# Moving the next loads to GpSimd's queue and the casts into one block in a fused attention and mixer kernel

## The chip, the cores and the metric

The kernel runs on one core of a Trainium2 chip. The time is the device time of one execution in microseconds, the median of several runs. The engines are TensorE (PE: matmuls and transposes), VectorE (DVE), ScalarE (ACT), GpSimd (POOL) and SyncE (SP). In this kernel SP issues most of the transfers and GpSimd the rest. Each engine works through its own list of instructions in the order in which the program gives them, and waits on semaphores for the others.

## The reference

There are B = 8 batches, H = 8 heads, S = 576 positions of head width D = 64, so that the model width is 512. `global_idx` names 8 of the positions as global. Inputs and output are float32.

```python
scores = scale * np.matmul(q, k.transpose(0, 1, 3, 2))
mask = np.abs(pos[:, None] - pos[None, :]) <= window          # window = 32
mask = mask | is_global[:, None] | is_global[None, :]
scores = np.where(mask, scores, -1000000000.0)
attn = np.exp(scores - np.max(scores, axis=-1, keepdims=True))
attn = attn / (np.sum(attn, axis=-1, keepdims=True) + 1e-09)
x = np.matmul(attn, v)            # heads side by side: (B, S, 512)
# mixer: token MLP across positions (576 -> 256 -> 576), channel MLP (512 -> 1536 -> 512)
h = np.maximum(xt @ w_tok1, 0.0) @ w_tok2                      # xt = x.transpose(0, 2, 1)
u = x + h.transpose(0, 2, 1)
h2 = np.maximum(u @ w_ch1, 0.0) @ w_ch2
return u + h2
```

So every position attends to a band of 65 neighbours and to the 8 global positions, and the global positions attend to everything. The result goes through the two MLPs.

## The kernel before, in words

All operands of matmuls are float16. The eight heads are taken as four pairs `p`, and the 576 positions as five tiles, the last of them with 64. The work is written out in *periods*: `period(b)` does the channel MLP of batch `b` and, between its pieces, the attention and the token MLP of batch `n = b + 1`. It also prepares batch `m = b + 2`.

- **Channel MLP.** The list `dense` holds units. `M4(b, j)` (12 of them) is four matmuls of 128x512 into a PSUM tile of the pool `psm`, which has two buffers, and a ReLU on ACT (L628). After an odd `b` three units `M4l` follow, which do the short last tiles of two batches. `M5(b, tau, part)` is six matmuls (L651). Part 1 ends in an add on DVE that makes `osb` (L655, L658 for the short tiles), and SP stores that. `d(k)` takes `k` units from the list. What a period leaves of the list is the `tail`, which the next period's `scores` take first.
- **Scores.** `scores(p)` has score matmuls (`S_`, L431) in the PSUM pool `pss` of three buffers, three exps on ACT (L444, L457, L462), and the mask products `SM` on DVE (L473 and L479). Between them stand units of `dense`. For the periods up to n = 2 `T` transposes the q and k of pair `p + 2` on PE into a `pss` buffer, and `TE` copies them to `qT` and `kT` (L414 to L420, all on DVE). From n = 3 on the transposes are DMAs (`turns`, on SP) and `order` copies their result to `kT` (L356) and `qT` (L362) on DVE.
- **Global positions.** `gather` and `gather_t` (L308 to L316) collect the global rows. `globals_` (L378) copies them into the first columns of each tile of `qT`. `GK` (L488) does the scores of the global positions for all pairs and `OG` their value products. `PV(n, tau)` are the value products of a tile.
- **Token MLP.** `M1`, `M2`, then `M3`, which transposes `u` into `uT` by DMAs on SP (for batch 0 by PE).
- **Loads and casts.** `load(i)` brings q and k of a batch as float32: `load_rest` into `lr`, `load_qk` into `lq` and `lk`, of which there is one buffer each. `casts` are nine float16 copies of these into `rn` and `qk` (L332, L335): `rn` first, then q and k of each pair. `load_v16` loads v on GpSimd with a cast in the transfer.

The order of the work is that of the program text on each engine. Within a period from n = 3 on it is: scores of pairs 0 to 2, `GK`, the `turns` of batch `m`, `load(m + 1)`, scores of pair 3, `OG`, the value products with `M1` and the `order` copies of batch `m`, `load_v16(m)`, `M2` and `M3`, the first three casts of batch `n + 2`, two units, and `globals_(m)`. The next six casts stand in the next period, three after `scores(0)` and three after `scores(1)`:

```python
        scores(0)
        cast(m, 3, 6)
        d(1 if tail > 5 else 0)
        scores(1)
        cast(m, 6, 9)
        d(max(tail - 4 - (tail > 5), 0))
        scores(2)
        GK(n)
```

Periods n = 1 and n = 2 differ: `load(2)` and `load(3)` stand at their heads, the casts of batch 2 are one block at the end of n = 1, those of batch 3 stand on GpSimd behind `GK(2)`, and `load(4)` follows the `turns` of batch 3.

Of the kernel before, what the change touches and what calls it, by code (L numbers as in the profile page):

```python
# [18 lines left out]
WIN = 32  # L19
# [7 lines left out]
def kernel(  # L27
# [12 lines left out]
    nc = tc.nc  # L40
    B, H, S, D = q.shape
# [7 lines left out]
    LAST = S - P * (NT - 1)  # L49
# [13 lines left out]
    def psm(shape, dtype=F32, name="m"):  # L63
        return psM.tile(shape, dtype, tag="m", name=name)
# [18 lines left out]
        r1 = P - WIN if c == NT - 1 else P  # L83
        return r0, r1, P * c - WIN + r0

    def load_qk(b, hs):
        for ten, dst in ((q, lq), (k, lk)):
            nc.sync.dma_start(
                out=dst[:, hs].rearrange("p h i d -> p h (i d)"),
                in_=ten[b, hs, 0 : S - LAST, :].rearrange("h (p i) d -> p h (i d)", i=4),  # L90
            )

    def load_rest(b):
        for t, ten in enumerate((q, k)):
            nc.sync.dma_start(
                out=lr[LAST * t : LAST * t + LAST], in_=ten[b, :, S - LAST : S, :].rearrange("h p d -> p h d")
            )

# [230 lines left out]
    def cast_qk(b, ti, p, eng):  # L329

        if p is None:
            eng(out=rn.rearrange("p n (r d) -> p (n r) d", r=2), in_=lr)  # L332
        else:
            hs = slice(2 * p, 2 * p + 2)
            eng(out=qk[:, ti, p].rearrange("q i (r d) -> q r i d", r=2), in_=(lq, lk)[ti][:, hs])  # L335

    def casts(b, eng):
        return [lambda: cast_qk(b, 0, None, eng)] + [
            lambda ti=ti, p=p: cast_qk(b, ti, p, eng) for p in range(NP) for ti in range(2)
        ]  # L340
# [36 lines left out]
    def globals_(b):  # L377
        nc.vector.tensor_copy(  # L378
            out=qTs[b % 2][:, :, :, 0:NG], in_=gT[:, b].unsqueeze(2).to_broadcast([P, NP, NT, NG])
        )  # L380
# [28 lines left out]
    def TE(b, p):  # L409
        pT = st[b]["pT", p]  # L410
        qT, kT = qTs[b % 2][:, p], kTs[b % 2][:, p]

        pm = pT[:, 0, 0:512].rearrange("p (i t x) -> p t x i", i=4, t=4)
        nc.vector.tensor_copy(out=qT[:, 0:4, GW:QS].rearrange("p t (x i) -> p t x i", i=4), in_=pm)  # L414
        nc.vector.tensor_copy(out=qT[:, 4, GW : GW + LAST], in_=pT[:, 1, 512 : 512 + LAST])
        nc.vector.tensor_copy(  # L416
            out=kT[:, WIN : WIN + 512].rearrange("p (x i) -> p x i", i=4),
            in_=pT[:, 1, 0:512].rearrange("p (i x) -> p x i", i=4),
        )
        nc.vector.tensor_copy(out=kT[:, WIN + 512 : WIN + S], in_=pT[:, 1, 512 + LAST : 640])  # L420

    def S_(b, p, part):
        qf = qTs[b % 2][:, p].rearrange("p t x -> p (t x)")
# [44 lines left out]
    def S_all(b, p):  # L468
        return S_(b, p, 0) + S_(b, p, 1)
# [74 lines left out]
    def M1(b, ch):  # L544
        s = st[b]
        if ch == 0 and b == 0:
            s["a1p"] = [psm([P, 512], name=f"a1p_{b}_{tt}") for tt in range(2)]
        elif ch == 0:
            ps = pss([P, 2, 512], name=f"a1p_{b}")
            s["a1p"], s["a1pp"] = [ps[:, 0], ps[:, 1]], ps  # L550
        ps = s["a1p"]
        for tt in range(2):
            w = w1[:, ch, P * tt : P * tt + P] if ch < NT - 1 else w1l[:, b % 2, P * tt : P * tt + P]
            nc.tensor.matmul(ps[tt], lhsT=w, rhs=x16s[b % 2][:, ch, :], start=(ch == 0), stop=(ch == NT - 1))  # L554
        if ch < NT - 1:
            return
        a1 = mb.tile([P, 2, DM], F16, tag="a1", bufs=1, name=f"a1_{b}")
        if b == 0:
            nc.scalar.activation(out=a1[:, 0], in_=ps[0], func=AF.Relu)
            nc.vector.tensor_scalar(out=a1[:, 1], in0=ps[1], scalar1=0.0, scalar2=None, op0=ALU.max)  # L560
        else:
            nc.scalar.activation(out=a1, in_=s["a1pp"], func=AF.Relu)
        s["a1"] = a1
        s["u16"] = mb.tile([P, 4, DM], F16, tag="u16", name=f"u16_{b}")
        if b % 2 == 0:
            s["ul"] = mb.tile([P, DM], F16, tag="ul", name=f"ul_{b}")
        else:
            s["ul"] = st[b - 1]["ul"]
# [20 lines left out]
    def M23_first(tau):  # L589
        s = st[0]  # L590
        if tau == 0:
            s["uT"] = mb.tile([P, 4, 512], F16, tag="uT", name="uT_0")
        ps = psm([P, 512], name=f"hp0_{tau}")
        for ch in range(2):
            nc.tensor.matmul(
                ps, lhsT=w2[:, ch, P * tau : P * tau + P], rhs=s["a1"][:, ch, :], start=(ch == 0), stop=(ch == 1)
            )
        nc.vector.tensor_add(out=s["u16"][:, tau], in0=x16s[0][:, tau], in1=ps)
# [8 lines left out]
    def M3(b, part):  # L607
        s = st[b]
        if part == 0:
            s["uT"] = mb.tile([P, 4, 512], F16, tag="uT", name=f"uT_{b}")  # L610
        if part < 2:
            for i in range(2):
                tau = 2 * part + i
                nc.sync.dma_start_transpose(out=s["uT"][:, :, P * tau : P * tau + P], in_=s["u16"][:, tau, :])
        else:
            s["uTl"] = mb.tile([P, 4, P], F16, tag="uTl", name=f"uTl_{b}")
            nc.sync.dma_start_transpose(out=s["uTl"], in_=s["ul"])
# [46 lines left out]
    def d(k):  # L664
        for _ in range(k):
            if dense:
                dense.pop(0)()

    def load(i):
        if i < B:  # L670
            load_rest(i)
            load_qk(i, slice(0, H))

    def turns(i):
        turn_rest(i)
        for p in range(NP):
            turn(i, p)

    def cast(i, lo, hi):
        if 3 < i < B:  # L680
            for c in casts(i, nc.scalar.copy)[lo:hi]:
                c()

    def period(b):
        n, m = b + 1, b + 2
        odd = b % 2
        dense.extend(lambda j=j: M4(b, j) for j in range(NJ))
        if odd:
            dense.extend(lambda j=j: M4l(b, j) for j in range(3))
        dense.extend(lambda t=t, i=i: M5(b, t, i) for t in range(4 + odd) for i in range(2))  # L690
        if n == B:
            d(len(dense))
            return
        tail = len(dense) - (23 if odd else 20) - 2 * odd
        regular = n > 2

        def scores(p):
            es = S_all(n, p)
            es[0]()
            es[1]()  # L700
            d(1)
            es[2]()
            if n < 3 and p < 2:
                T(n, p + 2)
            d(1)
            SM(n, p)
            if n < 3 and p < 2:
                TE(n, p + 2)
            elif n > 2 and p < 2:
                order(n, p + 2)  # L710

        if n == 1:
            load(2)
        elif n == 2:
            load(3)
        scores(0)
        cast(m, 3, 6)
        d(1 if tail > 5 else 0)
        scores(1)
        cast(m, 6, 9)  # L720
        d(max(tail - 4 - (tail > 5), 0))
        scores(2)
        GK(n)
        if regular and m < B:
            turns(m)
            load(m + 1)
        if n == 2:
            for c in casts(3, nc.gpsimd.tensor_copy):
                c()
            turns(3)  # L730
            load(4)
        d(1)
        scores(3)
        d(1)
        OG(n)
        d(1)
        if n == 3:
            gather_t(1)
        fill = [order_rest, lambda i: order_k(i, 0), lambda i: order_q(i, 0), lambda i: order_k(i, 1), lambda i: order_q(i, 1)]
        for tau in range(NT):  # L740
            PV(n, tau)
            if 0 < tau < 4:
                M1(n, tau - 1)
            if regular and m < B:
                fill[tau](m)
            if tau < 4:
                d(1)
        M1(n, 3)
        d(len(dense) - (8 + 2 * odd))
        M1(n, 4)  # L750
        d(1)
        if m < B:
            load_v16(m)
        M2(n, 0)
        M3(n, 0)
        M2(n, 1)
        M3(n, 1)
        M2(n, 2)
        if n % 2:
            M3(n, 2)  # L760
        if n == 1:
            for c in casts(2, nc.scalar.copy):
                c()
            d(2)
            T(2, 0)
            TE(2, 0)
            T(2, 1)
            TE(2, 1)
        else:
            cast(n + 2, 0, 3)  # L770
            d(1)
            if n == 2:
                order_rest(3)
                order(3, 0)
                order(3, 1)
            d(1)
        if m < B:
            globals_(m)

    def cast0(p):  # L780
        cast_qk(0, 0, p, nc.scalar.copy)
# [58 lines left out]
        M1(0, tau - 2)  # L840
    M1(0, NT - 2)
    M1(0, NT - 1)
    M23_first(0)
    M23_first(1)
    M3_first(0)
# [7 lines left out]
    T(1, 1)  # L853
    TE(1, 0)
    TE(1, 1)
    gather_t(0)
    globals_(1)
    qk_pads(1)
    pads(1)
    load_wc2(0)  # L860
# [36 lines left out]
```

## Time and profile before

| | |
|---|---|
| median of 3 runs | 349.94 us (348.34 to 350.1) |
| the profiled execution | 347.81 us |
| its span | 346.1 us |
| granted TensorE clock, mean | 0.982 |
| PE busy | 302.6 us (87%) |
| DVE busy | 200.6 us (58%) |
| ACT busy | 165.3 us (48%) |
| GpSimd busy | 72.3 us (21%) |

The span is what the trace covers; the execution's time includes what lies around it. In the trace's views a row of a timeline gives start, duration, engine, line and operation, then `out<-in`, the shapes, a count, and in brackets the idle time just before with what ended it. A row of the waits gives the waiting operation, what it waited for, and microseconds in all, times and the longest one. A row of the windows gives, for a stretch, its length, the busy time of PE, PE's weight loads, DVE, ACT and GpSimd with their counts, the granted clock, the DMA share and the rate in GB/s. Line numbers are those of the kernel before; the batch of a period is told from the time. S(n, p) stands for the score matmuls of batch n and pair p, e0(n, p) for their first exp, kT(n, p) and qT(n, p) for the copies, T(n, p) for the transposes on PE.

### The profile page before, as it was taken

The numbers are of one execution on the slowest core, as the hardware profiler recorded it, in microseconds if no ns is written. First come the engines' busy times: TensorE is split into PE (matmuls) and PEld (weight loads), VectorE is DVE, ScalarE is ACT, GpSimd is POOL, SyncE is SP. The second block draws the span as 40 slices with busy tenths as digits, with TensorE's granted clock in tenths as the row PEclk, the third lists the DMA queues.
The fourth block names the chain that finished last, engine by engine and source line by source line (L and its number), as shares of the span: only waits on it lengthen the run. The fifth ranks groups of instructions, "written<-read, shape, count | busy, mean of one in ns | idle before, by whom it ended". The sixth has DMA issues, their size and how long they took to land.

```text
span 346.1 us, 6451 instructions
## 1 busy us (share of the span) xinstructions
PE 302.6 (87%) x2541; PEld 157.8 (46%) x2541; DVE 200.6 (58%) x433; ACT 165.3 (48%) x292; POOL 72.3 (21%) x113
## 2 busy tenths in 40 slices
PE   1556859997989979999899999997899999998994
PEld 0334435553436634464346544643356445543641
DVE  5898767648396456675757456763763666351021
ACT  2438137605482346732973577335945247303600
POOL 8879535100069100040004000310000000000000
PEclk9999989999899989999999999999999999999998
DMA  5999999603889992599549964999350421033013
GB/s 156 255 294 155 225 247 196 39 32 91 239 186 127 228 229 76 108 127 296 150 112 134 290 128 102 112 226 238 93 93 17 110 77 30 0 76 123 0 63 91
DMA packets 114526, 48.18 MB, mean 139 GB/s; under 512 B 89408, under 2 KB 109760, under 8 KB 114496
## 3 DMA queue, kind: packets, MB, share of 16 engines
q1 hardware_dynamic: 77008, 39.60, 49.3%
q0 software_dynamic: 37200, 8.16, 29.1%
q8 instruction: 20, 0.33, 0.4%
q14 instruction: 10, 0.08, 0.1%
q10 hardware_dynamic: 288, 0.01, 0.0%
HBM read 36.12 MB, written 9.44 MB: 132 GB/s over the span
## 4 chain that ended last, share of the span: by engine, by line
PE 62%; DVE 16%; DMA 9%; ACT 7%; SPq 3%; issue 2%; ACTq 0%; DVEq 0%
PE op L651 21%; PE b1p L625 18%; DMA lk<-in_k_dram 8%; PE a1p L554 4%; PE s L431 3%; PE b1lp L638 3%; DVE e_all L479 3%; PE hp L578 3%; ACT e_all L444 3%; PE pv L531 2%; PE pv L522 2%; PE pv L527 2%; DVE kT L416 2%; ACT b L628 1%; ACT e_all L457 1%
## 5 line engine op out<-in xcount | busy, mean ns | idle before, releaser
L625 PE MATMUL b1p<-uT,wc 128*128 128x512 f16 x384 | 96.1, 383 | 5.4 <-DVE osb L655 4.3
L651 PE MATMUL op<-wc,b 128*128 128x512 f16 x384 | 90.8, 389 | 0.0
L628 ACT ACTIVATE b<-b1p 128x512 f16<-128x512 f32 x96 | 58.5, 609 | 64.9 <-PE b1p L625 64.6
L651 PEld LDWEIGHTS <-b 128*128 128x128 f16 x384 | 37.2, 99 | 45.8 <-issue 3.4
L625 PEld LDWEIGHTS <-wc 128*128 128x128 f16 x384 | 34.9, 98 | 48.5 <-issue 10.9
L655 DVE TENSOR_TENSOR osb<-u,op 128x512 f32<-128x512 f16 x32 | 21.9, 685 | 53.5 <-PE op L651 50.2
L324 POOL DMA_DIRECT2D vsh<-in_v_dram x35 | 29.9, 865 | 103.9 <-PE pv L531 101.1
L444 ACT ACTIVATE e_all<-s 128x832 f16<-128x832 f32 x32 | 27.8, 869 | 39.4 <-issue 20.6
L479 DVE TENSOR_TENSOR e_all<-e_all,bandm 128x1040 f16<-128x1040 f16 x64 | 43.7, 723 | 1.2
L584 DVE TENSOR_TENSOR u<-x,hp 128x512 f16<-128x512 f16 x28 | 17.4, 682 | 22.1 <-PE hp L578 22.1
L431 PE MATMUL s<-qT,kT 64*128 64x208 f16 (+1 forms) x320 | 20.9, 257 | 10.4 <-DVE qT L378 6.3
L539 DVE TENSOR_TENSOR x<-pv,rr 128x512 f16<-128x512 f32 (+1 forms) x40 | 27.6, 691 | 1.4
L522 PEld LDWEIGHTS <-e_all 128*128 128x128 f16 x320 | 22.1, 100 | 5.5 <-issue 0.5
L473 DVE TENSOR_TENSOR eg<-e_all,bandm 128x160 f16<-128x160 f16 x32 | 7.8, 245 | 28.8 <-ACT e_all L462 28.6
L522 PE MATMUL pv<-vsh,e_all 128*128 128x66 f16 x320 | 24.4, 197 | 0.0
L431 PEld LDWEIGHTS <-kT 64*128 64x128 f16 x320 | 12.5, 98 | 25.2 <-issue 16.1
L335 ACT CAST qk<-lq 128x512 f16<-128x512 f32 x28 | 17.8, 634 | 12.3 <-DMA lq<-in_q_dram 12.2
L457 ACT ACTIVATE e_all<-s 128x576 f16<-128x576 f32 x32 | 21.0, 657 | 3.2 <-PE s L431 3.2
L538 DVE RECIPROCAL rr<-pv 128x8 f32<-128x8 f32 (+1 forms) x40 | 8.3, 207 | 23.1 <-PE pv L531 22.9
L527 PE MATMUL pv<-vsh,e_all 128*128 128x66 f16 x256 | 21.1, 198 | 0.0
L335 ACT CAST qk<-lk 128x512 f16<-128x512 f32 x24 | 15.3, 638 | 11.6 <-DMA lk<-in_k_dram 11.6
L527 PEld LDWEIGHTS <-e_all 128*128 128x128 f16 x256 | 17.9, 101 | 3.5 <-issue 0.2
(154 smaller groups left out, 348.4 us busy)
## 6 DMA issues: line engine op xcount, KB each, us to landing
out_dram<-osb SPq DMA_DIRECT2D x32, 256.0 KB, 2.3
lq<-in_q_dram SPq DMA_DIRECT2D x7, 1024.0 KB, 7.4
lk<-in_k_dram SPq DMA_DIRECT2D x7, 1024.0 KB, 10.3
wc<-in_moe_w_ch_dram POOLq DMA_DIRECT2D x6, 512.0 KB, 12.9
vsh<-in_v_dram POOLq DMA_DIRECT2D x21, 128.0 KB, 5.8
vsh<-in_v_dram POOLq DMA_DIRECT2D x14, 96.0 KB, 6.2
lq<-in_q_dram SPq DMA_DIRECT2D x4, 256.0 KB, 5.3
lk<-in_k_dram SPq DMA_DIRECT2D x4, 256.0 KB, 5.7
```

Source lines behind the costliest of these rows:

```text
L324: nc.gpsimd.dma_start(out=vsh[b % 2][r0:r1, c, :, 0:D], in_=v[b, :, j0 : j0 + (r1 - r0), :].rearrange("h p d -> p h d"),)
L335: eng(out=qk[:, ti, p].rearrange("q i (r d) -> q r i d", r=2), in_=(lq, lk)[ti][:, hs])
L431: nc.tensor.matmul(ps[:, par, off : off + n], lhsT=kT[r, P * c : P * c + P], rhs=qf[r, lo : lo + n], start=True, stop=True,)
L444: nc.scalar.activation(out=e2[:, :, 1:3, 64:EW], in_=ps[:, :, 0 : 2 * W].rearrange("p h (c x) -> p h c x", c=2), func=AF.Exp, scale=scale,)
L457: nc.scalar.activation(out=o, in_=ps[:, :, 0 : 2 * QS].rearrange("p h (c x) -> p h c x", c=2), func=AF.Exp, scale=scale)
L479: nc.vector.tensor_mul(out=eh, in0=eh, in1=bandm)
L522: nc.tensor.matmul(o, lhsT=e_all[:, h, tau, EW - P - sh : EW - sh], rhs=vsh[b % 2][:, tau, h, :], start=hh == 0, stop=False,)
L527: nc.tensor.matmul(o, lhsT=e_all[:, h, tau + 1, 0:P], rhs=vsh[b % 2][:, tau + 1, h, :], start=False, stop=False)
L539: nc.vector.tensor_tensor(out=x16s[b % 2][r, tau, :].rearrange("p (f h x) -> p f h x", f=2, h=NP), in0=pq[r, :, :, 0:D], in1=rr[r].unsquee ...
L625: nc.tensor.matmul(ps, lhsT=wc1[:, cc, P * j : P * j + P], rhs=s["uT"][:, cc, :], start=(cc == 0), stop=(cc == 3))
L628: nc.scalar.activation(out=s["b1"][:, j, :], in_=ps, func=AF.Relu)
L651: nc.tensor.matmul(ps, lhsT=w, rhs=wc2[:, j, :], start=(j == 0), stop=(j == NJ - 1))
```

## The change

- Loads of q and k from batch 2 on are issued by GpSimd instead of SP. From n = 3 on `load(n + 2)` stands at the head of the period, ahead of the scores; before, it stood behind `GK` and the `turns`.
- The nine casts of batch `n + 2` stand in one block on ACT behind `M2` and `M3`. The casts of batch 2 (n = 1) stay where they were, those of batch 3 stay on GpSimd.
- `globals_(m)` moves from the end of the period to behind the value products, ahead of `M1(n, 3)`. `gather_t(0)` and `globals_(1)` move from behind the copies of batch 1's pairs 0 and 1 to ahead of `M23_first(0)`.
- The units of `dense` that stood behind `scores(0)` and `scores(1)` are taken inside `scores`, as `d(1 + k)` ahead of `SM` and of `TE` or `order`. The order on PE is the same; on DVE the `osb` add of such a unit comes ahead of the mask products and the copies.
- In `TE` the two `kT` copies of batches 1 and 2 are done by ACT instead of DVE.

```diff
--- before.py
+++ after.py
@@ -83,16 +83,16 @@
         r1 = P - WIN if c == NT - 1 else P
         return r0, r1, P * c - WIN + r0
 
-    def load_qk(b, hs):
+    def load_qk(b, hs, eng=None):
         for ten, dst in ((q, lq), (k, lk)):
-            nc.sync.dma_start(
+            (eng or nc.sync).dma_start(
                 out=dst[:, hs].rearrange("p h i d -> p h (i d)"),
                 in_=ten[b, hs, 0 : S - LAST, :].rearrange("h (p i) d -> p h (i d)", i=4),
             )
 
-    def load_rest(b):
+    def load_rest(b, eng=None):
         for t, ten in enumerate((q, k)):
-            nc.sync.dma_start(
+            (eng or nc.sync).dma_start(
                 out=lr[LAST * t : LAST * t + LAST], in_=ten[b, :, S - LAST : S, :].rearrange("h p d -> p h d")
             )
 
@@ -410,14 +410,15 @@
         pT = st[b]["pT", p]
         qT, kT = qTs[b % 2][:, p], kTs[b % 2][:, p]
 
+        copy_k = nc.vector.tensor_copy if b == 0 else nc.scalar.copy
         pm = pT[:, 0, 0:512].rearrange("p (i t x) -> p t x i", i=4, t=4)
         nc.vector.tensor_copy(out=qT[:, 0:4, GW:QS].rearrange("p t (x i) -> p t x i", i=4), in_=pm)
         nc.vector.tensor_copy(out=qT[:, 4, GW : GW + LAST], in_=pT[:, 1, 512 : 512 + LAST])
-        nc.vector.tensor_copy(
+        copy_k(
             out=kT[:, WIN : WIN + 512].rearrange("p (x i) -> p x i", i=4),
             in_=pT[:, 1, 0:512].rearrange("p (i x) -> p x i", i=4),
         )
-        nc.vector.tensor_copy(out=kT[:, WIN + 512 : WIN + S], in_=pT[:, 1, 512 + LAST : 640])
+        copy_k(out=kT[:, WIN + 512 : WIN + S], in_=pT[:, 1, 512 + LAST : 640])
 
     def S_(b, p, part):
         qf = qTs[b % 2][:, p].rearrange("p t x -> p (t x)")
@@ -668,18 +669,13 @@
 
     def load(i):
         if i < B:
-            load_rest(i)
-            load_qk(i, slice(0, H))
+            load_rest(i, nc.gpsimd)
+            load_qk(i, slice(0, H), nc.gpsimd)
 
     def turns(i):
         turn_rest(i)
         for p in range(NP):
             turn(i, p)
-
-    def cast(i, lo, hi):
-        if 3 < i < B:
-            for c in casts(i, nc.scalar.copy)[lo:hi]:
-                c()
 
     def period(b):
         n, m = b + 1, b + 2
@@ -694,7 +690,8 @@
         tail = len(dense) - (23 if odd else 20) - 2 * odd
         regular = n > 2
 
-        def scores(p):
+        def scores(p, k):
+
             es = S_all(n, p)
             es[0]()
             es[1]()
@@ -702,35 +699,27 @@
             es[2]()
             if n < 3 and p < 2:
                 T(n, p + 2)
-            d(1)
+            d(1 + k)
             SM(n, p)
             if n < 3 and p < 2:
                 TE(n, p + 2)
             elif n > 2 and p < 2:
                 order(n, p + 2)
 
-        if n == 1:
-            load(2)
-        elif n == 2:
-            load(3)
-        scores(0)
-        cast(m, 3, 6)
-        d(1 if tail > 5 else 0)
-        scores(1)
-        cast(m, 6, 9)
-        d(max(tail - 4 - (tail > 5), 0))
-        scores(2)
+        load(2 if n == 1 else 3 if n == 2 else n + 2)
+        scores(0, tail > 5)
+        scores(1, max(tail - 4 - (tail > 5), 0))
+        scores(2, 0)
         GK(n)
         if regular and m < B:
             turns(m)
-            load(m + 1)
         if n == 2:
             for c in casts(3, nc.gpsimd.tensor_copy):
                 c()
             turns(3)
             load(4)
         d(1)
-        scores(3)
+        scores(3, 0)
         d(1)
         OG(n)
         d(1)
@@ -745,6 +734,8 @@
                 fill[tau](m)
             if tau < 4:
                 d(1)
+        if m < B:
+            globals_(m)
         M1(n, 3)
         d(len(dense) - (8 + 2 * odd))
         M1(n, 4)
@@ -758,24 +749,23 @@
         M2(n, 2)
         if n % 2:
             M3(n, 2)
+        later = 2 if n == 1 else n + 2
+        if later < B:
+            for c in casts(later, nc.scalar.copy):
+                c()
         if n == 1:
-            for c in casts(2, nc.scalar.copy):
-                c()
             d(2)
             T(2, 0)
             TE(2, 0)
             T(2, 1)
             TE(2, 1)
         else:
-            cast(n + 2, 0, 3)
             d(1)
             if n == 2:
                 order_rest(3)
                 order(3, 0)
                 order(3, 1)
             d(1)
-        if m < B:
-            globals_(m)
 
     def cast0(p):
         cast_qk(0, 0, p, nc.scalar.copy)
@@ -840,6 +830,8 @@
         M1(0, tau - 2)
     M1(0, NT - 2)
     M1(0, NT - 1)
+    gather_t(0)
+    globals_(1)
     M23_first(0)
     M23_first(1)
     M3_first(0)
@@ -853,8 +845,6 @@
     T(1, 1)
     TE(1, 0)
     TE(1, 1)
-    gather_t(0)
-    globals_(1)
     qk_pads(1)
     pads(1)
     load_wc2(0)
```

## The prediction

> **What bounds the kernel now.** I read the page first: the busy shares, then the chain that ended last by engine.
>
> ```profile
> span 346.1 us, 6451 instructions
> PE 302.6 (87%) x2541; PEld 157.8 (46%) x2541; DVE 200.6 (58%) x433; ACT 165.3 (48%) x292; POOL 72.3 (21%) x113
> PE 62%; DVE 16%; DMA 9%; ACT 7%; SPq 3%; issue 2%; ACTq 0%; DVEq 0%
> ```
>
> TensorE (PE) is busy for 302.6 of 346.1 us, so the kernel is PE-bound with 43.5 us of gaps, and an edit is worth what it takes from or adds to those gaps, plus PE time at a low clock. The profiled execution took 347.81 us, 1.71 around its span; the median of the runs is 349.94, 2.13 above it. I sum against 347.81 and add 2.13 at the end. About 0.5% (1.75 us) is what a measurement here can tell from no change. Next I took the waits of PE, the windows by stage and the transfers in the chain:
>
> ```profile
> PE s L431 <- DVE qT L378: 6.3, 5, 2.7
> PE b1p L625 <- DVE osb L655: 4.3, 3, 1.6
> 200.00:228.00 28.00, 27.86 (x241) 14.02 (x240) 18.64 (x38) 17.07 (x33) 4.19 (x5) 1.00 0.81 118
> 154.21 10.12 DMA lk<-in_k_dram
> 226.70 11.18 DMA lk<-in_k_dram
> ```
>
> The first two rows (in all, times, longest) are waits that the diff touches: score matmuls waiting for the global columns (L378), and a channel-MLP unit waiting for a PSUM tile that a late `osb` add holds. The window row shows the other side: in the undisturbed period n=5 PE idles 0.14 of 28 us, so any new wait there is paid in full. The last two rows (issue, us to landing) say that the K load of periods 4 and 6 is itself in the chain.
>
> **Part 1: early loads and casts in one block (gain, n=4 and n=6).** ACT is in order. Before, the casts for the batch next but one stand there ahead of the exps of the period's first scores, and wait for a load issued late in the period before:
>
> ```profile
> 164.41 0.62 ACT L335 CAST qk<-lk 128x512 f16<-128x512 f32 x1 [2.79 <-DMA lk<-in_k_dram]
> 161.92 0.57 PE L431 MATMUL s<-qT,kT 64*128 64x208 f16 x10 [0.24 <-DVE qT L378]
> 165.84 0.39 PE L431 MATMUL s<-qT,kT 64*128 64x144 f16 x6 [0.36 <-ACT e_all L444]
> 173.26 1.02 PE L625 MATMUL b1p<-uT,wc 128*128 128x512 f16 x4 [1.57 <-DVE osb L655]
> 239.39 0.39 PE L431 MATMUL s<-qT,kT 64*128 64x144 f16 x6 [1.77 <-ACT e_all L444]
> 246.82 1.02 PE L625 MATMUL b1p<-uT,wc 128*128 128x512 f16 x4 [1.57 <-DVE osb L655]
> ```
>
> With the load issued at the head of period n, a whole period (about 35 us, from 161.92 to 234.07 are two) lies before its casts; the rows gave it 10 to 11. The casts then stand behind the token MLP, 9 x 0.52 (spacing of neighbouring casts) = 4.7 us, over before the next exps. The stalls on ACT go, and so does the 1.57, since the exps, the mask products and the `osb` adds are no longer late: n=4 gives 0.24 + 0.36 + 1.57 = 2.17, n=6 gives 0.24 + 1.77 + 1.57 = 3.58 (its 0.24 is the row below; it belongs to the moved global columns). Sum -5.75, between -3.3 (the two 1.57 and the 0.24s stay or turn into another wait) and -5.75. Nothing in n=5 and n=7, which have no such idles.
>
> **Part 2: global columns earlier (gain, n=2 and n=3).**
>
> ```profile
> 234.07 0.57 PE L431 MATMUL s<-qT,kT 64*128 64x208 f16 x10 [0.24 <-DVE qT L378]
> 123.22 0.57 DVE L356 COPY kT<-raw 128x512 f16<-128x512 f16 x1
> 124.22 0.19 DVE L378 COPY qT<-gT 128x160 f16<-128x160 f16 x1
> 124.45 0.57 PE L431 MATMUL s<-qT,kT 64*128 64x208 f16 x10 [2.26 <-DVE qT L378]
> 124.96 5.75 PE L651 MATMUL op<-wc,b 128*128 128x512 f16 x18
> 239.72 4.06 PE L651 MATMUL op<-wc,b 128*128 128x512 f16 x18
> ```
>
> At n=3 the first scores need pair 0 alone, whose copies end as pair 1's start (123.22, with some 0.1 of overlap); the columns at 124.22 stood behind both of pair 1's copies. Earlier columns let S(3,0) start about 1.15 sooner (124.45 - 123.30). The idle left is then 2.26 - 1.15 = 1.11, and the 18 matmuls behind it should run in 4.06 as at 239.72, not 5.75: another 1.69. Sum -2.84, between -1.15 and -2.84.
>
> A row and a rule on the clock: the idles of 2.26 (and 2.67, below) are followed by slow matmuls, the 1.77 at 239.39 is not, so the edge here lies between 1.77 and 2.26. The Trainium skill ("TensorE: Matmul & The Clock Gate", Part 1 and "HAM oscillation") has half clock only past about 3.4 us of idling, in a free-running window. By that rule the 1.69 would not be the idle's doing and would stay, -1.15 instead of -2.84; the rows differ from it, and I go by the rows.
>
> **Part 3: batches 1 and 2, K copies on ACT (loss).** In TE the K copies go from DVE to ACT, behind a wait for the DVE copies from the same PSUM tile; what queues behind them on ACT are the next exps and ReLUs, for which PE waits.
>
> ```profile
> 48.82 0.23 PE L309 MATMUL pg<-ident,g_q 128*128 128x128 f16 x1 [2.89 <-DVE g_q L308]
> 50.05 0.94 PE L431 MATMUL s<-qT,kT 64*128 64x208 f16 x10 [0.87 <-DVE qT L378]
> 45.17 0.68 DVE L587 TENSOR_TENSOR ul<-x,hp 64x512 f16<-64x512 f16 x1 [1.10 <-PE hp L578]
> 45.77 0.67 DVE L414 COPY qT<-pT 128x512 f16<-128x512 f16 x1
> 46.47 0.67 DVE L416 COPY kT<-pT 128x512 f16<-128x512 f16 x1
> 47.07 0.17 DVE L420 COPY kT<-pT 128x64 f16<-128x64 f16 x1
> 54.22 1.31 DVE L479 TENSOR_TENSOR e_all<-e_all,bandm 128x1040 f16<-128x1040 f16 x2
> 55.09 0.86 ACT L444 ACTIVATE e_all<-s 128x832 f16<-128x832 f32 x1
> 50.60:64.90 14.30, 14.02 (x110) 6.45 (x110) 8.56 (x20) 12.33 (x23) 7.23 (x8) 0.90 1.61 157
> ```
>
> Head of batch 1: the gather and the columns leave their place ahead of S(1,0) and go ahead of batch 0's `u`. That chain waits for PE here and there (1.10 before `ul`), so of the stretch that the gather takes now (48.82 to 50.05, 1.2) I let 0.8 through. Pair 0's Q copies then start at 45.77 + 0.8 and take 0.70 (to 46.47), its K copies on ACT 0.77 (46.47 to 47.24) and a hand-over of 0.1: S(1,0) at about 48.15 instead of 50.05, -1.9 (between 0 and the two idles' 3.76).
>
> Scores of batch 1: SM(1,0) ends on DVE at 54.22 + 1.31 = 55.5 and the Q copies 0.70 to 0.8 later, 56.3. Before, ACT went on with the next exp at 55.09; now it has kT(1,2) first and stands 1.2 longer, with the 0.7 of idle it had there 1.9. For kT(1,3) the same, 1.85. The two K pairs are about 0.8 each on ACT. That makes 1.9 + 1.85 + 1.6 = 5.3 us on an engine that in this window had 14.30 - 12.33 = 1.97 idle: +3.3, less the 1.9 head start. Net +1.4; up to +3.2 if the short PE idles that it brings (0.95 to 1.9) lower the clock. I take +2.1.
>
> ```profile
> 86.73 0.19 DVE L378 COPY qT<-gT 128x160 f16<-128x160 f16 x1
> 86.98 0.57 PE L431 MATMUL s<-qT,kT 64*128 64x208 f16 x10 [2.67 <-DVE qT L378]
> 87.48 2.63 PE L651 MATMUL op<-wc,b 128*128 128x512 f16 x6
> 90.87 1.55 PE L651 MATMUL op<-wc,b 128*128 128x512 f16 x6
> 92.45 0.69 DVE L655 TENSOR_TENSOR osb<-u,op 128x512 f32<-128x512 f16 x1 [5.53 <-PE op L651]
> 93.72 0.61 PE L405 MATMUL pT<-ident,qk 128*128 128x128 f16 x8
> ```
>
> Batch 2: S(2,0) no longer waits for the columns at 86.73 and the copies split on two engines: 85.45, -1.53; its following 6 matmuls in 1.55 rather than 2.63, -1.08. All later work of PE would come 2.6 earlier. But kT(2,2) on ACT now follows `osb` (92.45 - 2.6 = 89.9), SM (1.5), the Q copies (0.7) and is 0.8 itself: with the add's 0.6 it ends at 93.5, and the transposes T(2,3) need the PSUM buffer that it frees. PE reaches them at 93.72 - 2.6, some 91.2, and idles 2.3. The gain is spent there. Then kT(2,3) holds ACT in the same way behind SM(2,1), and the exps of pair 2 come some 1.8 late, part of it hidden. Net +1.0 by the value products, between -1.5 and +3.
>
> **Part 4: extra output units ahead of the mask products (loss, n=3 to 7).** `d(1 + k)` puts the tail's `osb` adds ahead of SM and `order` on DVE. The fourth pair of GK's matmuls waits for the second `order` copy.
>
> ```profile
> 206.85 0.69 DVE L655 TENSOR_TENSOR osb<-u,op 128x512 f32<-128x512 f16 x1 [1.98 <-PE op L651]
> 209.46 0.60 DVE L362 COPY qT<-raw 128x512 f16<-128x512 f16 x1
> 209.33 0.57 PE L431 MATMUL s<-qT,kT 64*128 64x208 f16 x10
> 211.66 0.36 PE L488 MATMUL gk<-qT,kgz 128*32 128x384 f16 x4
> ```
>
> From the start of an `osb` to the end of that copy: 209.46 + 0.60 - 206.85 = 3.21. Now this chain begins when the last output unit ends on PE (T0, here about 209.4) plus 0.2, and ends at T0 + 3.4; PE wants GK's fourth pair at T0 + 2.3 to 2.6 (211.66 is T0 + 2.3, three of its matmuls first). A stall of about 0.83 (0.83 to 1.1) in each of five periods, in which PE has no slack: +4.2 (4.2 to 5.5; 0 if DVE starts the add earlier than PE's modelled end). It's a wait that before is not there at all.
>
> **Part 5: the queue.** 24 load issues leave SP for Pool. Pool's v loads bound their price.
>
> ```profile
> L324 POOL DMA_DIRECT2D vsh<-in_v_dram x35 | 29.9, 865 | 103.9 <-PE pv L531 101.1
> ```
>
> Four issues of 0.87 are 3.5 us a period on an engine that waits 100 us; load(n+2) waits there for the casts of n+1, and only load_v16 queues behind it, not wanted for a period. So the issue costs nothing; without that cover it would be 3.5 a period. What changes is the company: the loads (10.12 and 11.18 to landing above) now run beside the `uT` transposes and the output stores at a period's start. I add +0.5 (0 to +4: `uT` is issued about 6 us or more ahead of its use).
>
> **Sum.** 347.81 - 5.75 - 2.84 + 2.1 + 1.0 + 4.2 + 0.5 = 347.0; on the median's level 349.1, -0.2%.
>
> **Rivals.**
> R1, faster: the new waits are covered. The `order` chain of part 4 needs to be only 0.8 us quicker, and DVE idles nearby (1.98 before the `osb`). Without part 4, 344.9; with batches 1 and 2 near their lower ends too, 343. Against: the chain is made of rows.
> R2, slower: the clock. Part 3 makes idles of 1.85 to 2.3 where the trace's edge is 1.77 to 2.26. If they count as long, each costs 1.69 as at 124.96: three of them +5.1, 354.2. It decides from about 2 us of idle. For: 2.3 is past 2.26. Against: the windows' clock already dips to 0.90 there with little idle.
> R3, slower: the loads on Pool land late or hold up `uT`. The new bound is then the end of +4: 352.6. For: 11.18 us for one transfer before. Against: a period to land. A page bears on this: the Trainium skill ("DMA: Bandwidth & Descriptors", "SWDGE vs HWDGE vs iDMA") says that GpSimd's descriptors are written to SBUF state from which VectorE's two-port modes lock it out, and that SP's are immune. By that rule the issues would stretch; the v rows' 0.87 beside a DVE busy 58% don't show it.
> R4, it doesn't do what it says: the DMA waits on ACT come back because a load waits for its buffer: part 1 is lost, 354.8.
>
> **How the numbers follow.** Forecast as summed 0.45, R1 0.22, R2 0.18, R3 0.10, R4 0.05. The forecast's own range, from the bounds of parts 1 to 4 taken half to each side, is 346.5 to 352. Of its 0.45, 0.13 lies under 348.2 (0.5% faster), 0.25 between, 0.07 above 351.7. Faster: 0.22 + 0.13 = 0.35. Same: 0.25 and 0.02 of R3 = 0.27. Slower: 0.07 + 0.18 + 0.08 + 0.05 = 0.38. The range of 8 in 10 runs from half of R1 to R2: 344.0 to 354.5.
>
> **What would show it.** In the changed profile: no cast on ACT waiting for a load in n=4 and n=6; no score matmul waiting for L378's global columns; 18 matmuls behind S(3,0) in about 4.06; a new wait of GK's matmuls for the `order_q` copy, 0.8 a period; ACT's K copies waiting for DVE in batches 1 and 2 and PE transposes waiting for them. Wrong would be: no wait at GK (then R1), PE clock under 0.9 between 85 and 117 us (R2), matmuls of `uT` waiting for a transfer (R3), casts still waiting (R4).

## The result and the profile after

The changed kernel takes 362.39 us (median of 4 runs, 361.49 to 362.76) against 350.02 for the kernel before (4 runs, 348.34 to 351.37). The ratio is 1.0352 with a 95% interval of 1.0303 to 1.0401: slower by 3.5%, outside the range of the forecast. The profiled execution took 361.49, its span is 359.8, 13.7 more than before. The page of the changed kernel, its busy shares and the chain that ended last:

```profile
span 359.8 us, 6482 instructions
PE 307.7 (86%) x2541; PEld 158.9 (44%) x2541; DVE 194.4 (54%) x417; ACT 171.7 (48%) x308; POOL 92.5 (26%) x137
PE 63%; DVE 17%; DMA 8%; ACT 5%; issue 4%; SPq 2%; DVEq 0%; ACTq 0%
```

PE has 52.1 us of gaps instead of 43.5, and 5 us more of busy time for the same 2541 matmuls, which is a lower clock (granted 0.962 in the mean, 0.982 before). Its waits say where (what waits, for what; us in all, times, longest):

```profile
PE b1p L626 <- issue: 4.9, 1, 4.9
PE b1p L626 <- DVE osb L656: 4.3, 3, 2.4
PE b1p L626 <- DMA uT<-u: 3.3, 1, 3.3
PE b1p L626 <- ACT b L629: 2.7, 2, 1.3
PE gk L489 <- ACT kT L421: 1.9, 2, 1.1
PE gk L489 <- DVE qT L362: 1.7, 3, 0.6
PE s L432 <- DVE qT L362: 1.2, 1, 1.2
```

No row has L378, the global columns, any more, and no cast ahead of the scores' exps holds PE up. In their place the first channel-MLP matmuls (L626) wait. The third row names the transposed `u`. The first says "issue", but the view of the line that issues those transposes (L615) puts the same wait on the weight load ahead of that matmul, and gives the landing times:

```profile
  PEld L626: 5.1, 1
  PE b1p L626: 3.3, 1
DMA to landing us min/median/max: 2.4/2.6/10.6
```

So PE waits twice for `uT`, in periods 2 and 4. Two long transfers stand in the chain of the changed kernel (start, us):

```profile
169.23 10.61 DMA uT<-u
214.11 8.46 DMA out_dram<-osb
```

The timeline of its PE shows what ended behind them, with the idle time in brackets:

```profile
97.85 1.86 PE L626 MATMUL b1p<-uT,wc 128*128 128x512 f16 x4 [4.88 <-issue]
179.97 1.87 PE L626 MATMUL b1p<-uT,wc 128*128 128x512 f16 x4 [3.33 <-DMA uT<-u]
223.41 3.56 PE L626 MATMUL b1p<-uT,wc 128*128 128x512 f16 x8 [2.40 <-DVE osb L656]
```

Its timelines of SP and GpSimd at the first of these places:

```profile
83.43 5.93 SPq L615 DMA_TRANSPOSE uT<-u  x4
86.03 0.90 POOL L88 DMA_DIRECT2D lq<-in_q_dram  x1 [2.24 <-ACT qk L335]
86.91 0.89 POOL L88 DMA_DIRECT2D lk<-in_k_dram  x1
```

And its timeline of DVE at the third:

```profile
222.67 0.69 DVE L656 TENSOR_TENSOR osb<-u,op 128x512 f32<-128x512 f16 x1 [4.70 <-DMA out_dram<-osb]
```

GpSimd comes to a load at the moment when ACT's cast block has freed the buffers, and that block stands next to `M3`, so the load starts while the `uT` transposes are under way (83.43 on SP, 86.03 on GpSimd). The last transpose of period 2 is issued at 87.44 and takes 10.3 to land; PE wants it at 92.97 (97.85 - 4.88). Late landings as such are not new. In the kernel before, the view of the same line (L614) has

```profile
DMA to landing us min/median/max: 2.4/3.4/8.4
```

but there no matmul waits for them. In period 5 the last `uT` lands as late (issued at 211.87, 10.0), but what ends PE's wait is an `osb` add held up by an output store that takes 8.46: the three `osb` buffers are full, DVE waits 4.70 for one, and PE waits for the PSUM tile that DVE would free. Behind each of these three idles of 2.4 to 4.9 the matmuls are slow: 1.86 or 1.87 for 4 and 3.56 for 8, where 1.02 and 1.90 are usual.

### The profile page after: what moved, and what is told of

Same layout as the page of the kernel before. It is cut to its first block, busy times and chain, and to the rows that moved or that the text cites. A ratio compares the mean times of both kernels' runs of the same rounds, so it can differ in the third digit from the quotient of the medians.

```text
span 359.8 us, 6482 instructions
## 1 busy us (share of the span) xinstructions
PE 307.7 (86%) x2541; PEld 158.9 (44%) x2541; DVE 194.4 (54%) x417; ACT 171.7 (48%) x308; POOL 92.5 (26%) x137
## 3 DMA queue, kind: packets, MB, share of 16 engines
q0 software_dynamic: 41040, 22.32, 38.9%
## 4 chain that ended last, share of the span: by engine, by line
PE 63%; DVE 17%; DMA 8%; ACT 5%; issue 4%; SPq 2%; DVEq 0%; ACTq 0%
PE b1p L626 20%; PE op L652 19%; PE a1p L555 4%; PE hp L579 4%; DVE e_all L480 4%; DMA out_dram<-osb 4%; PE b1lp L639 3%; DMA uT<-u 3%; PE pv L523 3%; PE s L432 3%; PE pv L532 3%; PE pv L528 2%; ACT e_all L445 2%; DVE osb L656 2%; DMA lk<-in_k_dram 2%
## 5 line engine op out<-in xcount | busy, mean ns | idle before, releaser
L626 PE MATMUL b1p<-uT,wc 128*128 128x512 f16 x384 | 102.6, 404 | 15.9 <-issue 4.9
L652 PE MATMUL op<-wc,b 128*128 128x512 f16 x384 | 87.9, 379 | 0.0
L626 PEld LDWEIGHTS <-wc 128*128 128x128 f16 x384 | 36.7, 102 | 62.9 <-issue 28.4
L480 DVE TENSOR_TENSOR e_all<-e_all,bandm 128x1040 f16<-128x1040 f16 x64 | 42.6, 707 | 1.2
L95 POOL DMA_DIRECT2D lr<-in_q_dram x6 | 4.3, 713 | 95.3 <-ACT rn L332 95.3
L555 PE MATMUL a1p<-x,w 128*128 128x512 f16 x64 | 18.9, 379 | 0.0
```

Of the source, the lines that this page charges most:

```text
L480: nc.vector.tensor_mul(out=eh, in0=eh, in1=bandm)
L626: nc.tensor.matmul(ps, lhsT=wc1[:, cc, P * j : P * j + P], rhs=s["uT"][:, cc, :], start=(cc == 0), stop=(cc == 3))
L652: nc.tensor.matmul(ps, lhsT=w, rhs=wc2[:, j, :], start=(j == 0), stop=(j == NJ - 1))
```

## The experiments

The twelve runs start from the changed kernel (`a_`, `d_`) or from the kernel before (`b_`). Ratios are to the kernel before, run on the same chip; spans, waits and landings are those of one profiled execution of each kernel. What the table shows is worked out from the starts of S(n,0) in the timeline of PE: the length of each period, with what the prediction's steps make of it if part 5 (the +0.5) is left out.

| us | before | forecast without part 5 | changed | a_noload | a_dvek_noload |
|---|---|---|---|---|---|
| head, to S(1,0) | 50.05 | 48.15 | 48.72 | 48.65 | 49.17 |
| n=1 | 36.93 | 39.4 | 39.99 | 38.86 | 33.72 |
| n=2 | 37.47 | 38.9 | 43.21 | 39.67 | 34.60 |
| n=3 | 37.47 | 36.4 | 36.47 | 36.47 | 36.47 |
| n=4 | 37.14 | 36.0 | 41.78 | 35.80 | 35.81 |
| n=5 | 35.01 | 35.6 | 38.83 | 35.71 | 35.70 |
| n=6 | 38.54 | 36.0 | 35.81 | 35.80 | 35.80 |
| from S(7,0) | 73.49 | 74.3 | 74.99 | 74.34 | 74.13 |
| span | 346.1 | 344.8 | 359.8 | 345.3 | 335.4 |

**a_noload: what do the loads cost?**

```diff
-        if i < B:
+        if i < 3:
             load_rest(i, nc.gpsimd)
```

> The changed kernel without the loads of q and k of batches 3 to 7 (what was loaded last is cast again; that part of the data is left out). It prices everything that these loads cost beside other transfers. Theory 1: 12 to 16 us faster than the changed kernel, 346 to 350: no wait of PE for uT in periods 2 and 4, none for an osb add in 5. Theory 3 (the K copies on ACT and the order of DVE): at most 4 us faster, over 358.

347.88 us, ratio 0.9963 (0.9937 to 0.9989); span 345.3, 14.5 less than the changed kernel. The waits of its PE have no row for `uT`, and an `osb` add holds PE 1.0 us in all:

```profile
PE b1p L626 <- ACT b L629: 3.5, 4, 1.3
PE gk L489 <- DVE qT L362: 2.9, 5, 0.6
PE b1p L626 <- DVE osb L656: 1.0, 1, 1.0
```

Theory 1 holds: at their new place the loads cost 14.5 us, most of it in periods 1, 2, 4 and 5 of the table (1.1, 3.5, 6.0 and 3.1). PE is busy 302.9 us here, so 4.8 of the 14.5 are slower matmuls and 9.7 are gaps. The run leaves the loads out altogether; it prices the loads at this place and on this queue, and doesn't tell the one from the other. The changed kernel's other periods, and all of a_noload's, are within 0.8 us of the prediction's steps.

**a_dvek: what do the K copies on ACT cost?**

```diff
-        copy_k = nc.vector.tensor_copy if b == 0 else nc.scalar.copy
+        copy_k = nc.vector.tensor_copy
```

> The changed kernel with one edit: the K copies of batches 1 and 2 go back to DVE. Theory 1 (two causes: the loads on GpSimd's queue collide with the uT transposes and the output stores in periods 2, 4 and 5, some 13 to 16 us; the K copies on ACT cost some 5 us in periods 1 and 2, by the idles 0.49 + 0.40 + 0.83 + 1.34 and 1.11 + 1.34 and low clock behind them): 3 to 5 us faster than the changed kernel, about 358. Theory 2 (the loads account for all of it): within 1 us of the changed kernel. Theory 3 (the K copies on ACT are most of it): 8 us faster or more, under 354.

354.68 us, ratio 1.0186 (1.0121 to 1.0251); span 352.0, 7.8 less. More than theory 1 had, less than theory 3 asked for. In the changed kernel the waits of ACT have this row (12.2 us over 6 copies):

```profile
ACT kT L417 <- DVE qT L416: 12.2, 6, 4.3
```

The longest is in period 2, in ACT's timeline of the changed kernel:

```profile
95.48 0.58 ACT L417 COPY kT<-pT 128x512 f16<-128x512 f16 x1 [4.30 <-DVE qT L416]
```

In the 4.30 ACT does nothing, because its next instruction is a copy whose partner on DVE stands behind an `osb` add and the mask products. With the copies on DVE period 1 takes 34.18 instead of 39.99 (S(2,0) starts at 82.36, S(1,0) at 48.18). Period 4 takes 1.4 more than in the changed kernel, with a wait for `uT` of 3.90 instead of 3.33, so the 7.8 is a net.

**a_dvek_noload: do the two costs add?** Both edits together.

> The changed kernel with both: K copies on DVE and no loads of q and k of batches 3 to 7 (that data is left out). It shows whether the two costs add. If they do: span 359.8 - 7.8 (a_dvek) - 14.5 (a_noload) = 337.5, time about 339 to 340. If they hide each other in period 2 (the wait for uT stands where the K copies' wait stands): more is gained by both than by the sum there, since either alone leaves the other wait in place, 334 to 337; if what one frees the other had already freed: 342 or more.

337.51 us, ratio 0.9646 (0.9605 to 0.9686); span 335.4. The sum of the two single gains would be 337.5 in span; 2.1 more is gained. That is the way of the second expectation, though 337.51 lies just above its 334 to 337. Its reason, two waits that hide each other in period 2, accounts for 1.4 us (period 2 gains 8.6 by both, 3.5 and 3.7 singly); as much again is in period 4, where a_dvek alone lost. So the loads and the K copies account for 24.4 us. The span is 10.7 under that of the kernel before, but this kernel also lacks the loads that the kernel before has to carry, so how much of it the rest of the change gains isn't shown here.

**a_sp and a_dvek_sp: the same places, on SP's queue.**

```diff
-            load_rest(i, nc.gpsimd)
-            load_qk(i, slice(0, H), nc.gpsimd)
+            load_rest(i)
+            load_qk(i, slice(0, H))
```

> The changed kernel with one edit: the loads at the same places of the program, but on SP's queue, where they stand behind the uT transposes of the period before. Theory 1a (the queue decides: in one queue the transposes land first, on GpSimd's the loads share the transfer engines with them): the waits of PE for uT in periods 2 and 4 (4.88 and 3.33) go with their low clock, 8 to 12 us faster than the changed kernel, 350 to 354; the output stores now queue behind the loads, so some wait for an output buffer may grow. Theory 1b (the place decides, not the queue: loads right at the time of the transposes collide on whatever queue): within 3 us of the changed kernel.

358.97 us, ratio 1.0301 (1.0242 to 1.036); span 356.6. PE waits for no `uT` any more (its longest landing is 6.8), so theory 1a has that wait right. But the gain is 3.2 in span and not 8 to 12, close to the 3 that theory 1b allowed, and the intervals of the two ratios overlap. The wait moves. The loads are now ahead of other things in the one queue and behind SP's waits. So the queue alone is worth some 3 of the 14.5; the other 11.3 are paid on SP's queue too, in other waits. The casts of batch 4 wait for a load that took 15.94, and hold up the exps behind them; in period 5 the stores queue behind the load. The timeline of PE of a_sp:

```profile
134.41 0.60 PE L432 MATMUL s<-qT,kT 64*128 64x144 f16 x6 [3.27 <-ACT e_all L445]
220.70 1.87 PE L626 MATMUL b1p<-uT,wc 128*128 128x512 f16 x4 [4.07 <-DVE osb L659]
```

> The changed kernel with the K copies on DVE and the loads of q and k at the same places on SP's queue. Theory 1a (behind the transposes in one queue the loads don't slow them): no wait for uT; what is left is the cast block's wait for load(4) in period 3 (3.27 in a_sp) and the stores behind the loads in period 5 (4.07 in a_sp): 5 to 9 us faster than a_dvek, 345 to 350. Rival: with the two batches' copies quicker, the loads meet more of the transposes, same as a_dvek.

354.76 us, ratio 1.0103 (1.005 to 1.0157), which overlaps with a_dvek's: the expectation of 5 to 9 us missed. Both waits grew, to 7.63 and 5.20, as the load was met earlier.

**a_dvek_actq: ACT's queue.** The same edit with `nc.scalar`.

> The changed kernel with the K copies on DVE (a_dvek, span 352.0) and the loads of q and k at the same places on ACT's queue. Theory A (any queue other than SP's runs beside SP's transposes and stores and slows them): the waits for uT (4.74 and 3.90) and for the osb add (2.54) stay within 1.5 us each, 349 to 355; ACT pays for four issues a period besides. Theory B (it is GpSimd's queue, with descriptors made by software, that slows them): the waits for uT go, 340 to 345.

355.92 us, ratio 1.0147 (1.0105 to 1.019). It doesn't decide between A and B. A wait for `uT` is left in period 2 (2.93), the one in period 4 is gone; and ACT itself now waits behind its load issues, which costs PE 4.05 behind a ReLU in period 2, and 2.54 and 2.40 behind the exps of periods 4 and 5. Whether software-made descriptors matter stays open.

**a_oldorder: the order on DVE.**

```diff
-            d(1 + k)
+            d(1)
             SM(n, p)
...
                 order(n, p + 2)
+            d(k)
```

> The changed kernel with one edit: the extra output units stand behind the mask products and the copies again, as before the change. Theory 1: the waits of GK's matmuls for the second order copy (0.57, 0.58 and 0.58 in periods 3, 6 and 7) go, 1.7 us faster than the changed kernel or a little less. Rival: the osb adds that then come late hold the PSUM tile for the next channel-MLP unit as before (1.57 each in periods 4 and 6): 0 to 3 us slower.

360.82 us, ratio 1.0354 (1.0296 to 1.0412): no difference. Three waits of GK's matmuls, 1.7 us in all, go, and the wait for `osb` adds in period 5 grows from 2.40 to 3.53 + 1.23. Both expectations were half right: periods 3 and 6 get 1.0 shorter, period 5 gets 3.0 longer.

**b_globals: the columns alone.**

```diff
+        if m < B:
+            globals_(m)
         M1(n, 3)
...
-        if m < B:
-            globals_(m)
...
     M1(0, NT - 1)
+    gather_t(0)
+    globals_(1)
     M23_first(0)
```

> The kernel before with one part of the change alone: the global columns ahead of M1(n, 3), and the gather with the columns of batch 1 ahead of batch 0's u. Theory 1: the score matmuls of batches 1, 2, 3, 4 and 6 no longer wait for L378. The waits were 2.89 + 0.87 (of which 1.2 to 1.9 go), 2.67 (only 0.3, as the K copies on DVE end right before the columns), 2.26 (1.15, with 1.69 of low clock behind it), 0.24 twice: 4.5 to 5.5 us faster than before, about 345. Rival: the clock stays low behind the idle of 1.1 that is left in period 3, and the waits for the loads, now reached earlier, take the gain back: 0 to 3 us faster.

345.18 us, ratio 0.990 (0.987 to 0.993). The time is theory 1's 345, but not by its sum. S(3,0) starts at 115.82 instead of 124.45, 8.6 sooner where 4.5 to 5.5 were expected, and only 3.9 of this is left in the span (342.2): the late load catches it, in the timeline of PE of b_globals:

```profile
124.50 0.60 PE L431 MATMUL s<-qT,kT 64*128 64x144 f16 x6 [3.84 <-ACT e_all L444]
235.61 0.39 PE L431 MATMUL s<-qT,kT 64*128 64x144 f16 x6 [2.72 <-ACT e_all L444]
```

The second row says something of the clock too: behind an idle of 2.72 the six matmuls run at full speed, 0.39.

**b_pool: the queue alone**, with the casts split as before, so that GpSimd comes to the load behind `scores(1)`.

```diff
-            load_rest(i)
-            load_qk(i, slice(0, H))
+            load_rest(i, nc.gpsimd)
+            load_qk(i, slice(0, H), nc.gpsimd)
```

> The kernel before with one part of the change alone: the loads of q and k from batch 2 on are issued by GpSimd, at the same places of the program, with the casts split as before. GpSimd comes to a load as soon as the casts that free its buffers are done, here after scores(1) and not at the end of the period before, so the uT transposes are through by then. Theory 1 (what hurts is that the loads run at the same time as the uT transposes and the output stores): no wait of PE for uT; the casts' waits for the loads in periods 4 and 6 go (2.17 and 3.58), 3 to 6 us faster than before, 344 to 347. Rival (loads on GpSimd's queue hurt whatever runs on SP's, here the transposes of q and k): the order copies on DVE and with them the value products wait, slower than before.

348.79 us, ratio 1.0011 (0.998 to 1.0041). Both mechanisms are there, and neither time: the gain of theory 1 and the loss of the rival leave it where it was. The casts' waits in periods 4 and 6 go. One wait for `uT` is there against theory 1, in the timeline of PE of b_pool at the start of period 2:

```profile
94.24 1.02 PE L625 MATMUL b1p<-uT,wc 128*128 128x512 f16 x4 [1.85 <-issue]
```

The profile names no releaser, but the last `uT` transpose, issued at 83.72, takes 10.4 and lands 0.1 before this start. The load now also meets the transposes of q and k, whose median landing goes from 2.8 to 7.3, and DVE's `order` copies wait for them. The view of those transposes (L349) in the kernel before:

```profile
DMA to landing us min/median/max: 2.4/2.8/6.4
```

and in b_pool, with who waited for them first:

```profile
  DVE kT L356: 9.0, 5
DMA to landing us min/median/max: 2.4/7.3/11.5
```

**d_gate: the changed kernel with the load held back to GK**, K copies on DVE, load(3) on SP.

```diff
+            gate = tiny.tile([P, GW], F16, tag="gate", name=f"gate_{n}")
+            nc.gpsimd.tensor_copy(out=gate, in_=eg[:, 0, 4, :])
+            load(n + 2)
         GK(n)
```

> The changed kernel with the K copies on DVE (a_dvek), load(3) on SP, and from period 3 on the load on GpSimd behind a small copy of a result of SM(n, 2), so that it is issued at the time of GK, past the uT transposes. Theory 1: the waits for uT (4.74 with 0.8 of low clock, and 3.90 with some 2.4) and the wait for an osb add in period 5 (2.54) go: 10 to 14 us faster than a_dvek, 341 to 345. Rival (what the loads run beside matters little, they slow down whatever transposes there are): the transposes of q and k at GK are late in their turn, the order copies hold up DVE in the value products, 0 to 5 us faster than a_dvek.

Its four runs lie between 342.6 and 354.2 (median 347.91), too far apart for its time to decide anything. Its profile (span 345.3) has no wait for `uT`, and the transposes of q and k land in a median of 8.9: the rival's late turn is there, and PE waits 3.67 for it in the token MLP of period 5 (225.68).

**b_shift and b_shift45: another way to the same end.** b_globals, loads as before on SP behind the transposes, and no cast ahead of the first scores' exps. b_shift45 puts four casts behind `scores(0)` and five behind `scores(1)`:

```diff
         scores(0)
-        cast(m, 3, 6)
+        cast(m, 0, 4)
...
         scores(1)
-        cast(m, 6, 9)
+        cast(m, 4, 9)
...
-            cast(n + 2, 0, 3)
```

> The kernel before with the earlier global columns and gather of b_globals, loads as before on SP behind the transposes, and the casts of batch n + 2 all in the next period, three each behind scores(0), scores(1) and scores(2), so that no cast stands ahead of the first scores' exps. Theory 1: the casts' wait for the loads then no longer holds up the exps of the first scores: 4 to 6 us faster than b_globals, 339 to 341. Rival: the casts meet the late load behind scores(0) all the same and hold up the exps of scores(1), or three casts ahead of GK hold up ACT's ReLUs: within 2 us of b_globals.

341.59 us, ratio 0.9809 (0.9753 to 0.9866): 0.9 points under b_globals, the way of theory 1 but 3.6 us and not 4 to 6. Three casts ahead of GK leave waits for the ReLUs (0.75 + 0.76 in each of periods 5 and 6).

> b_shift (span 339.2) with four casts behind scores(0) and five behind scores(1) and none ahead of GK. Theory: the waits of PE for ACT's ReLUs in periods 4, 5 and 6 (0.55 + 0.76, 0.75 + 0.76, 0.75 + 0.76) go: 3 to 4 us faster than b_shift, about 338. Rival: the five casts hold up the exps of scores(2) and with them the osb adds: within 1 us of b_shift.

337.57 us (5 runs, 337.04 to 340.62), ratio 0.9633 (0.9598 to 0.9668): faster than either kernel, by 3.7% than the one before, as the theory had it. The profiled execution is the slowest of the five (340.62). In the waits of its PE those for the ReLUs are down to 0.7 in all:

```profile
PE b1p L625 <- ACT b L628: 0.7, 3, 0.3
```

The late load(4) still costs in period 3, by its PE's timeline:

```profile
130.81 1.86 PE L625 MATMUL b1p<-uT,wc 128*128 128x512 f16 x4 [1.59 <-DVE osb L655]
133.91 1.86 PE L625 MATMUL b1p<-uT,wc 128*128 128x512 f16 x4 [1.24 <-DVE osb L658]
```

## Why the prediction was wrong

**Part 5, the queue, is the step that failed.** It was put at +0.5 with an upper end of +4, and measured 14.5: the forecast without it takes the loads as costing nothing, which is what a_noload measures. What it said of the issue was right: 0.90 and 0.89 on an idle GpSimd. The "company" was mis-sized in three ways. First, it set the lead of `uT` ("about 6 us or more") against no landing time under load, though the kernel before already had one of 8.4. In period 2 the last transpose is issued 5.5 ahead of its use and takes 10.3. Second, the sum bounded `uT` alone and gave the stores no price. They hold three `osb` buffers, and one store of 8.46 stopped DVE and PE in period 5. Third, the matmuls behind these waits are slow, some 4.8 us by PE's busy time. The rows that could have warned were there: the load's place on GpSimd isn't the period's head in the text but the moment when the casts free its buffers, so the cast block's place sets the load's. The prediction named that wait, and didn't ask what runs at that moment. That the queue as such does the harm isn't shown: on SP's queue the same places cost 11.3 of the 14.5 (a_sp), and the queue changed alone, at the places of the kernel before, leaves the time where it was (b_pool).

**Rival R3 is what happened**, with a price of 352.6 where 362.4 was measured, and a chance of 0.10. The issues are not stretched beside a busy DVE: 0.90 and 0.89, where the `v` loads before took 0.87. So the rule of the Trainium skill that the prediction cites there ("DMA: Bandwidth & Descriptors", "SWDGE vs HWDGE vs iDMA") shows no sign here. The Trainium skill ("DMA: Bandwidth & Descriptors", "Issuing engines are not separate DMA queues") says that transfers from whatever engine run on the same 16 transfer engines and interleave. The trace agrees as far as it goes: SP's `uT` transposes take up to 10.6 beside GpSimd's loads, and at most 3.6 in a_noload, without most of them.

**Parts 1 and 2 came out.** No cast holds up PE in n=4 and n=6, no score matmul waits for L378, and in the changed profile (PE's timeline) the 18 matmuls behind S(3,0) run in full clock behind an idle of 1.15, as forecast:

```profile
131.92 0.57 PE L432 MATMUL s<-qT,kT 64*128 64x208 f16 x10 [1.15 <-DVE qT L362]
132.42 4.06 PE L652 MATMUL op<-wc,b 128*128 128x512 f16 x18
```

In the table n=3 to n=6 of a_noload lie within 0.3 of the forecast. But a_noload has no loads that a cast could wait for, so part 1 is shown by the changed kernel's n=6 (35.81); its n=4 has the wait for `uT`. The lower end of part 1, -3.3, doesn't follow from its own words: without the two 1.57 and the two 0.24, 2.13 is left. The 1.69 of part 2 came out partly by luck, for the edge of the clock between 1.77 and 2.26 doesn't hold. In b_pool's timeline of PE the same idle of 2.26 at the same place is followed by full speed:

```profile
125.15 0.57 PE L431 MATMUL s<-qT,kT 64*128 64x208 f16 x10 [2.26 <-DVE qT L378]
125.65 4.06 PE L651 MATMUL op<-wc,b 128*128 128x512 f16 x18
```

So is the 2.72 in b_globals, while 1.59 in b_shift45 and 2.40 in the changed kernel are followed by slow matmuls. The idle's length alone doesn't decide; what does is not shown here.

**Part 3 was right in sum.** Periods 1 and 2 of a_noload take 78.5 together, forecast 78.3 (39.4 and 38.9; measured 38.9 and 39.7). The idle of 2.3 ahead of the transposes T(2,3), worked out from rows, is there in a_noload's timeline of PE:

```profile
95.04 0.61 PE L405 MATMUL pT<-ident,qk 128*128 128x128 f16 x8 [2.29 <-ACT kT L421]
```

In the changed kernel the wait for `uT` stands just ahead of these transposes and hides it. In the paragraph on the head of batch 1 the times in brackets (46.47, 47.24) leave out the 0.8 that its result, 48.15, has in it. But the net of +3 hid two large terms, which the single runs show: the columns alone bring S(3,0) 8.6 forward (b_globals), and the K copies on ACT cost 7.8 of span in the changed kernel.

**Part 4 was right in size.** The wait of GK's matmuls is 0.57 and not 0.83 (five times, 2.9 in all, in a_noload; in periods 4 and 5 of the changed kernel it hides behind the other waits). But with the old order periods 3 and 6 are 1.0 shorter (a_oldorder), so the order costs there about what was forecast; in period 5 it saves 3.0.

**The other rivals.** R2's sign is just there: the clock between 85 and 117 us is 0.89 in the changed kernel. One of the slow stretches in it stands behind the wait for `uT` (97.85), the other behind an idle of 1.34 (106.77, 1.33 for 4 matmuls). In a_noload slow matmuls stand behind part 3's 1.69 and 2.29, and the two periods still take what was forecast, so R2 isn't what made the 362.4. R1 and R4 are out: GK's matmuls wait, and no cast waits for a load in n=4 and n=6.

Without part 5 the forecast is 346.5 for the profiled run; a_noload's took 347.05.

## What to carry to other kernels

A transfer on a queue of an engine that has nothing else to do starts when its buffer comes free, wherever the program text puts it: look for what runs at that moment, above all transposes by DMA and stores with few buffers, and price it at the landing time under load. Before a copy goes to another engine, look at what queues behind it there: here the K copies on ACT stood ahead of the exps, and waited up to 4.30 for DVE. If a late load holds up a busy engine, moving the waiting step a few instructions back can be worth more than bringing the load forward (b_shift45, ratio 0.9633, against 0.990 for b_globals, on which it builds).

## What the runs showed of the hardware

DMA transposes issued by SP land in a median of 2.4 us, at most 3.6, where the loads of batches 3 to 7 are left out (`uT`, a_noload). While two loads of 1 MB run on GpSimd's queue they take up to 10.6 (`uT`, the changed kernel) or a median of 7.3 and 8.9 (q and k, b_pool and d_gate). Behind loads on SP's own queue single ones take as long: 8.4 in the kernel before, 12.5 in a_dvek_sp, but there PE waits for none of them. With the loads on ACT's queue one of the two waits stayed (2.93). Which property of the queue decides isn't settled. Nor is the clock's rule: in one profiled execution an idle of 1.59 us is followed by slow matmuls (b_shift45), in another one of 2.72 is not (b_globals).
